# Attention followed by soft MoE and an MLP on one core: remainder-chunk sums and v product as 64x64 corner products, with the maxima and VectorE's long steps spread over other groups

## The chip, the cores and the metric

One core of a Trainium2 chip runs the whole program in one launch. The metric is device time in microseconds (us); lower is better. Times of this kernel differ from run to run by about 0.3%.

## The reference

Only the attention at the front is touched by the change; what follows it (a soft mixture of experts and a two-layer MLP) is unchanged.

```python
def _attn_ref(q, k, v):                   # (4, 8, 576, 64): batch, heads, sequence, head dim
    q_rot, k_rot = rotate(q), rotate(k)   # rotary embedding
    scores = 1/sqrt(64) * q_rot @ k_rot.T
    scores = scores - max(scores, -1)
    attn = exp(scores)
    attn = attn / (sum(attn, -1) + 1e-9)
    return attn @ v
```

All in float32. The attention's output, transposed to (2304, 512), goes into the MoE, and that one's output into the MLP.

## The kernel before

The 32 heads are taken as 16 **pairs** p, each of two heads hd. The 576 query columns of a pair are taken in two **halves** h of 288. The 576 keys of each head make four chunks of 128, and the two remainders of 64 keys (one a head) are put together into one more chunk of 128 rows, the **remainder chunk**, c = 4: rows 0 to 63 are the first head's, rows 64 to 127 the second's. The attention is thus a list of 16 x 2 x 5 = 160 **groups** (p, h, c), with c in the order 4, 0, 1, 2, 3. I number the ten groups of a pair i = 0 to 9: i = 0 is the remainder chunk of the first half, i = 1 to 4 its four whole chunks, i = 5 the remainder chunk of the second half, i = 6 to 9 its whole chunks.

For each group the loop issues, in this order:

- `scores` (L380 to L404): TensorE makes the transposed scores st (keys on the partitions, 288 queries) in float32r, two products for each head (L398 and L399; for the remainder chunk L387 and L388, twice), and ScalarE takes the exponential into the tile e (L400; er, L389, for the remainder chunk). Three PSUM buffers hold st.
- A **maximum unit** (`max_unit`, `max_reduce`, L335 to L361). The maximum of each query's scores is needed before the exponentials, so it is found two pairs ahead: nine units u = 0 to 8 for a pair. A unit is a product with the difference of the two halves of the keys (kd, made by `k_diff`, L335, on VectorE), a relu on ScalarE (L351), a product with the second half of the keys, and one VectorE step (L360) that adds the two and reduces them to a maximum. Each of the two products has one PSUM buffer (mx0, mx1): the next unit's first product must wait for ScalarE's relu, its second for VectorE's step. Unit 4 has two products in place of each. `MAX_AT` says how many units stand in each of the ten groups from group 40 on; before that `MAX_COUNTS` does.
- `esum` (L405 to L417): GpSimd (POOL) adds up e of the four whole chunks into es (L412, then L417 twice), and, with c = 1, the remainder chunk: its rows 0 to 63 onto the first head's (L414), rows 64 to 127 onto the second's (L415).
- `session`: at i = 0 and 5 the product with v, `pv` (L419 to L427), of the chunks 4, 0 and 1 of the half before; at i = 2 and 7 that of the chunks 2 and 3, and then `sums` (L431 to L439), products of es with ones that put each query's sum s on 64 partitions. Products of whole chunks are 128 x 64 (L426, L435): one for each head, with 64 columns of the array each, in float32, which shows as two records for each product. The product of the remainder chunk with v is 128 x 128, with zeros in the two corners that would mix the heads (L423).
- the tasks that a table puts at this group (`at`, `first`): the normalization `norm` (L446, L447, with `NORM`) and `norm2` (L453), the transposed output `x_t` (L465, `X_T`), the rotary steps of a later pair (`ROT`, in order f0 and f1 products L270 and L273, f2 sum L276, f3 rounding L280, m0 copies by DMA, f4 difference L285, m2), `k_diff` (`K_DIFF`), weight conversions (L149 to L155), loads. f0, f2 and f4 run on VectorE, one step a head, f1 on POOL.

All engines run their instructions in the order in which they were issued, so this order is the schedule.

Of the kernel before, what the change touches and what calls it, by code (L numbers as in the profile page):

```python
# [12 lines left out]
ALU = mybir.AluOpType  # L13
# [25 lines left out]
ROT_2 = (-26, -22, -19, -21, -23, -19, -19, -18, -18, -18, -17, -18, -17)  # L39
ROT_3 = (-31, -25, -27, -26, -26, -24, -23, -23, -22, -16, -22, -19, -15)  # L40
ROT_4 = (-28, -28, -26, -28, -24, -23, -23, -20, -22, -17, -19, -21, -17)
ROT = (-28, -27, -24, -24, -24, -23, -22, -22, -21, -20, -20, -19, -19)
Q_COPY = -6
V_LOAD = -6
K_DIFF_2 = -14
K_DIFF_3 = -15
K_DIFF_4 = -16
K_DIFF = -17
QK_LOAD = -34
QK_LOAD_3 = -54  # L50
QK_LOAD_4 = -31
# [2 lines left out]
MAX_ROW_2 = -4  # L54
MAX_ROW_3 = -5
RECIP = 7
NORM = 8
NORM2 = 9
X_T = ((21, 25), (15, 20), (15, 20), (15, 20))
W_IN_AT = (9, 20, 30, 40, 49, 60, 70, 81, 89, 100, 110, 120)  # L60
W_IN_STEPS = (1, 2, 5)
FETCH_AHEAD = 5
# [1 line left out]
W_LOADS = (30, 52, 62, 70, 65, 81, 81, 74, 105, 95, 118, 135, 127, 143, 127, 132, 133, 134, 140, 153)  # L64
SCALES = -19
EARLY = -10
MAX_AT = (0, 1, 1, 1, 1, 1, 1, 1, 1, 1)
MAX_FROM = (6, 2, 6)
MAX_COUNTS = (0, 1, 2, 2, 2, 2, 0, 0, 1, 1, 1, 1, 1, 2, 2, 0, 1, 1, 1, 1, 1, 1, 1, 1, 1, 2, 1, 1, 1, 1, 1, 1, 1, 1, 2, 1, 1, 1, 1, 1)

# [5 lines left out]
def attn_softmoe_mlp_kernel(ctx: ExitStack, tc: tile.TileContext, qk, v, cst, phi, w1, w2, w_in, w_out, out):  # L76
    nc = tc.nc
    pe, act, dve, pool, sp = nc.tensor, nc.scalar, nc.vector, nc.gpsimd, nc.sync
# [13 lines left out]
    ones = const.tile([128, 64], F32, tag="ones", name="ones")  # L92
# [99 lines left out]
    with tc.manual_schedule():  # L192
        with ExitStack() as t1:
# [25 lines left out]
            raw, vt = {}, {}  # L219
# [156 lines left out]
            et = {}  # L376
            u_ps = {}
# [27 lines left out]
            es = {}  # L405

            def esum(p, h, c):
                e = et[p, h, c]
                add = (dve if p == NPAIR - 1 and h == 1 else pool).tensor_tensor
                if c == 1:  # L410
                    t = es[p, h] = (p1 if h else es0).tile([128, 2, HS], F32, tag="es", name=f"es{p}_{h}")
                    add(out=t, in0=et[p, h, 0], in1=e, op=ALU.add)  # L412
                    r = et[p, h, 4]
                    add(out=t[0:64, 0], in0=t[0:64, 0], in1=r[0:64], op=ALU.add)  # L414
                    add(out=t[64:128, 1], in0=t[64:128, 1], in1=r[64:128], op=ALU.add)  # L415
                elif c in (2, 3):
                    add(out=es[p, h], in0=es[p, h], in1=e, op=ALU.add)  # L417

            def pv(p, h, c):  # L419
                e = et[p, h, c]  # L420
                if c == 4:
                    u_ps[p, h] = ps_u.tile([128, HS], F32, tag="u", name=f"u{p}_{h}")
                    pe.matmul(u_ps[p, h], lhsT=vt[p][:, 4, :], rhs=e, start=True, stop=False, skip_group_check=True)  # L423
                    return
                for hd in range(2):
                    pe.matmul(u_ps[p, h][64 * hd:64 * hd + 64, :], lhsT=vt[p][:, c, 64 * hd:64 * hd + 64], rhs=e[:, hd],  # L426
                              start=False, stop=c == 3, skip_group_check=True)  # L427
# [3 lines left out]
            def sums(p, h):  # L431
                wp, tag = (ps_mx, "mx1") if (p, h) == (NPAIR - 1, 1) else (ps_m, "m")
                s = wp.tile([128, HS], F32, tag=tag, name=f"s{p}_{h}", **({"bufs": 1} if wp is ps_mx else {}))
                for hd in range(2):
                    pe.matmul(s[64 * hd:64 * hd + 64, :], lhsT=ones, rhs=es[p, h][:, hd], start=True, stop=True)  # L435
                rs[p, h] = p1.tile([128, HS], F32, tag="rs", name=f"rs{p}_{h}")
                r0[p, h] = p1.tile([128, HS], F32, tag="r0", name=f"r0{p}_{h}")
                act.activation(out=rs[p, h], in_=s, func=ACTF.Ln, bias=eps)
                es[p, h] = s  # L439
# [4 lines left out]
            def norm(p, h):  # L444
                r, q, s = rs[p, h], r0.pop((p, h)), es.pop((p, h))
                dve.scalar_tensor_tensor(out=s, in0=s, scalar=EPS, in1=q, op0=ALU.add, op1=ALU.mult)  # L446
                dve.scalar_tensor_tensor(out=r, in0=s, scalar=-2.0, in1=q, op0=ALU.add, op1=ALU.mult)  # L447
# [179 lines left out]
            def at(g, *fs):  # L627
                tasks.setdefault(g, []).extend(fs)

            def first(g, f):  # L630
                tasks.setdefault(g, []).insert(0, f)
# [33 lines left out]

            ROTARY = [([r[i] for r in (ROT_2, ROT_3, ROT_4, ROT)], k, a) for i, (k, a) in enumerate(((8, ()), (0, (0,)), (1, (0,)), (1, (1,)), (0, (1,)), (2, (0,)), (2, (1,)), (3, (0, act)), (3, (1, act)), (5, ()), (4, (0,)), (4, (1,)), (6, ())))]

            for p in range(NPAIR):
                g0 = 10 * p
                if p >= 1:  # L670
                    at(g0 + Q_COPY, rt(p, 7))
                if p >= 2:
                    for o, k, a in ROTARY:
                        at(g0 + o[min(p, 5) - 2], rt(p, k, *a))
                    at(g0 + V_LOAD, lambda p=p: load_v(p))
                    first(g0 + (K_DIFF_2, K_DIFF_3, K_DIFF_4, K_DIFF)[min(p, 5) - 2], lambda p=p: k_diff(p))
                if p >= 3:
# [8 lines left out]
                    at(g0 + 11, lambda: hb.append(half(1)), lambda: hb[3][0]((0, 1, 2)))  # L686
                for h in range(2 * (p < NPAIR - 1)):
                    first(g0 + 5 * h + RECIP, lambda p=p, h=h: recip(p, h))
                    at(g0 + 5 * h + NORM, lambda p=p, h=h: norm(p, h))
                    at(g0 + 5 * h + NORM2, lambda p=p, h=h: norm2(p, h))  # L690
                for i in range(2 * (p < NPAIR - 1)):
                    at(g0 + X_T[p % 4][i], lambda p=p, i=i: x_t(p, i))
# [77 lines left out]
            g0, g1, g2, g3, g4 = rot[1][0:5]  # L770
# [38 lines left out]
            for g in range(NG + 2):  # L809
                i = g % 10  # L810
                if g < NG:
                    p, h, c = groups[g]
# [35 lines left out]
            t = ps_u.tile([128, HS], F32, tag="u", name="lt3_ps")  # L848
# [43 lines left out]
        op = {}  # L892
# [227 lines left out]
    with tc.manual_schedule():  # L1120
        (wf0, _), (wf1, n1) = first
        dummy(1)
        t = ps_o.tile([128, 512], F32, tag="o", name="g0_ps")[:, 0:128]
# [23 lines left out]
    for n, (j, k) in enumerate(seq):  # L1147
        ghi, glo = gt.pop((j, k))
        for i in range(NI):
            if k == 0:  # L1150
                ops[j, i] = ps_o.tile([128, DM], F32, tag="o", name=f"ops{j}_{i}")
            t = ops[j, i]
# [61 lines left out]
```

## Time and profile before

| | |
|---|---|
| time, median of 3 runs | 689.65 us (688.49 to 690.51) |
| time of the profiled execution | 687.64 us |
| its span, all instructions | 685.8 us |
| mean granted TensorE clock | 0.95 |
| attention's first remainder exponential to its last group | about 27 us to 386 us of the span |
| busy: TensorE, VectorE, ScalarE, POOL | 611.0, 413.4, 360.9, 280.8 us |

The profile is one execution of the program. Busy time counts a matmul up to the end of its pipeline, so TensorE can be counted busy while its array already stands free. A granted clock of 1 is 2.4 GHz, 0.5 is 1.2 GHz. "[0.41 <-ACT relu L351]" behind a row says that the engine stood idle for 0.41 us before it and that ScalarE's step of line 351 ended this.

### The profile page before, as it was taken

What the parts mean: (1) busy time and instruction counts of PE and PEld (TensorE: products, weight loads), DVE (VectorE), ACT (ScalarE), POOL (GpSimd) and SP (SyncE); (2) the same over time, 40 slices, a digit from 0 to 9 for tenths busy, and PEclk for the clock granted to TensorE, in tenths of its full rate; (3) what the DMA queues carried; (4) which work ended last, traced back from release to release, by engine and by line L of the source; (5) the groups of instructions that cost most, each with busy time, mean ns of one, the idle gap of its engine ahead of it and who ended that gap; (6) DMA issues with size and microseconds to landing.
All of it is one profiled execution on the core that took longest, in us unless ns stands there. A gap on an engine that the chain in (4) does not pass through costs nothing.

```text
span 685.8 us, 10364 instructions
## 1 busy us (share of the span) xinstructions
PE 611.0 (89%) x3443; PEld 422.1 (62%) x3443; DVE 413.4 (60%) x866; ACT 360.9 (53%) x920; POOL 280.8 (41%) x226
## 2 busy tenths in 40 slices
PE   4688879889889789888998999998889999999997
PEld 2465655566556456555665533366668888888886
DVE  6686667785577666677824424267895544454443
ACT  2464655674566456466755522068775443454432
POOL 5476587966577665778747200001340000000000
PEclk9579999998799988999999999999999999999999
DMA  6885668865869775577696369983430200020002
GB/s 211 208 228 154 177 174 223 226 168 181 221 181 246 236 207 151 189 193 214 162 328 232 115 246 387 392 331 125 155 99 1 93 0 1 0 93 1 0 1 92
DMA packets 43190, 113.86 MB, mean 166 GB/s; under 512 B 4977, under 2 KB 6273, under 8 KB 41345
## 3 DMA queue, kind: packets, MB, share of 16 engines
q1 hardware_dynamic: 42956, 112.87, 54.1%
q8 instruction: 27, 0.44, 0.3%
q10 hardware_dynamic: 180, 0.34, 0.2%
q14 instruction: 27, 0.21, 0.1%
HBM read 78.12 MB, written 7.60 MB: 125 GB/s over the span
## 4 chain that ended last, share of the span: by engine, by line
PE 63%; DVE 14%; ACT 9%; issue 7%; DMA 5%; ACTq 1%; POOL 1%; SPq 0%; DVEq 0%; POOLq 0%
PE u L426 9%; PE ops L1155 8%; PE ops L1156 8%; PE ops L1154 8%; PE psmx L346 6%; PE st L398 4%; PE l L899 3%; PE st L399 3%; DVE raw L270 2%; ACT relu L351 2%; DVE relu L360 2%; PE s L435 2%; DMA w_out_raw<-in_w_out_dram 2%; PE l L878 2%; PE hps L1049 2%
## 5 line engine op out<-in xcount | busy, mean ns | idle before, releaser
L360 DVE CUSTOM_DVE_ANT_0 relu<-psmx,relu 128x288 f32<-128x288 f32 x144 | 65.2, 454 | 99.7 <-ACT relu L351 75.8
L400 ACT ACTIVATE e<-st 128x288 f32<-128x288 f32 x256 | 101.5, 410 | 23.5 <-PE st L399 22.3
L1155 PE MATMUL ops<-wo_lo,ghi 128*128 128x512 f32 x288 | 112.3, 390 | 0.5 <-POOL wo_lo L1032 0.5
L1154 PE MATMUL ops<-wo_hi,ghi 128*128 128x512 f32 x288 | 112.7, 392 | 0.0
L1156 PE MATMUL ops<-wo_hi,glo 128*128 128x512 f32 x288 | 112.5, 391 | 0.0
L417 POOL TENSOR_TENSOR es<-es,e 128x576 f32<-128x576 f32 x62 | 102.9, 1660 | 9.4 <-ACT e L400 5.0
L1056 DVE TENSOR_TENSOR hps<-hps,g 128x384 f32<-128x384 f32 x96 | 49.9, 560 | 81.5 <-ACT g L1053 81.3
L398 PE MATMUL st<-sa,sa 128*128 128x288 f32 x256 | 88.4, 347 | 1.0 <-ACT er L389 0.6
L1053 ACT ACTIVATE g<-hps 128x384 f32<-128x384 f32 x96 | 42.6, 490 | 81.8 <-PE hps L1049 81.4
L426 PE MATMUL u<-e,v 128*64 128x288 f32 x512 | 85.5, 457 | 0.0
L412 POOL TENSOR_TENSOR es<-e,e 128x576 f32<-128x576 f32 x31 | 45.1, 1456 | 92.5 <-ACT e L400 92.4
L399 PE MATMUL st<-qb,kb 65*128 65x288 f32 x256 | 78.9, 310 | 0.0
L346 PE MATMUL psmx<-sa,sa 128*128 128x288 f32 x160 | 55.2, 362 | 25.0 <-DVE mx L360 24.9
L351 ACT ACTIVATE relu<-psmx 128x288 f32<-128x288 f32 x144 | 58.8, 410 | 29.1 <-DVE mx L360 20.6
L346 PE MATMUL psmx<-kd,sa 128*128 128x288 f32 x160 | 54.3, 356 | 22.0 <-ACT relu L351 14.8
L398 PEld LDWEIGHTS st<-sa,sa 128*128 128x128 f32 x256 | 51.8, 202 | 20.0 <-issue 15.8
L1156 PEld LDWEIGHTS ops<-wo_hi,glo 128*128 128x128 f32 x288 | 54.1, 188 | 11.7 <-issue 0.2
L1155 PEld LDWEIGHTS ops<-wo_lo,ghi 128*128 128x128 f32 x288 | 54.1, 188 | 10.6 <-POOL wo_lo L1032 0.8
L1154 PEld LDWEIGHTS ops<-wo_hi,ghi 128*128 128x128 f32 x288 | 54.0, 188 | 9.6 <-issue 0.2
L1032 POOL TENSOR_TENSOR wo_lo<-wf,wo_hi 128x512 fp32r<-128x512 f32 x14 | 20.1, 1437 | 89.1 <-DMA w_out_raw<-in_w_out_dram 51.5
L426 PEld LDWEIGHTS u<-e,v 128*64 128x64 f32 x512 | 33.3, 148 | 34.6 <-issue 22.8
L346 PEld LDWEIGHTS psmx<-kd,sa 128*128 128x128 f32 x160 | 32.4, 209 | 35.3 <-ACT relu L351 26.5
(191 smaller groups left out, 1072.5 us busy)
## 6 DMA issues: line engine op xcount, KB each, us to landing
w<-in_w_dram SPq DMA_DIRECT2D x64, 512.0 KB
sa<-raw SPq DMA_DIRECT2D x56, 288.0 KB
raw<-in_qk_dram SPq DMA_DIRECT2D x13, 1152.0 KB
w_out_raw<-in_w_out_dram SPq DMA_DIRECT2D x16, 512.0 KB
w_in_raw<-in_w_in_dram SPq DMA_DIRECT2D x12, 512.0 KB
v<-in_v_dram SPq DMA_DIRECT2D x15, 320.0 KB
qb<-sa SPq DMA_DIRECT2D x16, 288.0 KB
out_dram<-os SPq DMA_DIRECT2D x18, 256.0 KB
```

What stands on the lines that cost most here:

```text
L346: pe.matmul(t, lhsT=rem_cols(qa, hd, 128) if u == 4 else qa[:, c0:c0 + 128], rhs=k, start=u != 4 or hd == 0, stop=u != 4 or hd == 1)
L351: act.activation(out=r, in_=t, func=ACTF.Relu)
L360: dve.tensor_tensor_reduce(out=r, in0=mxt.pop((p, u, 1)), in1=r, scale=1.0, scalar=-3.0e38, op0=ALU.add, op1=ALU.max, accum_out=mx[p][:, u ...
L398: pe.matmul(st, lhsT=ka[:, c0:c0 + 128], rhs=qa[:, o:o + HS], start=True, stop=False)
L399: pe.matmul(st, lhsT=kb[0:65, c0:c0 + 128], rhs=qb[0:65, S * hd + HS * h:S * hd + HS * h + HS], start=False, stop=True)
L400: act.activation(out=e[:, hd], in_=st, func=ACTF.Exp, scale=0.125)
L417: add(out=es[p, h], in0=es[p, h], in1=e, op=ALU.add)
L426: pe.matmul(u_ps[p, h][64 * hd:64 * hd + 64, :], lhsT=vt[p][:, c, 64 * hd:64 * hd + 64], rhs=e[:, hd], start=False, stop=c == 3, skip_grou ...
L1056: dve.tensor_tensor(out=t[i], in0=t[i], in1=g[i], op=ALU.mult)
L1154: pe.matmul(t, lhsT=a, rhs=wo_hi[k], start=k == 0, stop=False)
L1155: pe.matmul(t, lhsT=a, rhs=wo_lo[k], start=False, stop=False)
L1156: pe.matmul(t, lhsT=b, rhs=wo_hi[k], start=False, stop=k == 15)
```

## The change

Three things change. The remainder chunk no longer goes through POOL's adds: its sums are two more products in `sums`, each 64 x 64, from rows 0 to 63 to partitions 0 to 63 and from rows 64 to 127 to partitions 64 to 127, accumulated onto those of es. The remainder chunk's product with v becomes two 64 x 64 products in the same corners. And numbers in the tables move: the group without a maximum unit is i = 4 and no longer i = 0, `norm` of the first half goes to i = 9 from i = 8, `k_diff` to i = 4 from i = 3, the second `x_t` to one group later, and of the rotary steps f0 of the first head goes from i = 3 to i = 5, f1 of the first head from i = 6 to i = 5, m0 from i = 0 to i = 9.

```diff
-ROT = (-28, -27, -24, -24, -24, -23, -22, -22, -21, -20, -20, -19, -19)
+ROT = (-28, -25, -25, -24, -24, -23, -22, -22, -21, -21, -20, -19, -19)
...
-K_DIFF = -17
+K_DIFF = -16
...
-NORM = 8
+NORM = (9, 8)
 NORM2 = 9
-X_T = ((21, 25), (15, 20), (15, 20), (15, 20))
+X_T = ((21, 25), (15, 21), (15, 21), (15, 21))
...
-MAX_AT = (0, 1, 1, 1, 1, 1, 1, 1, 1, 1)
+MAX_AT = (1, 1, 1, 1, 0, 1, 1, 1, 1, 1)
...
                     add(out=t, in0=et[p, h, 0], in1=e, op=ALU.add)
-                    r = et[p, h, 4]
-                    add(out=t[0:64, 0], in0=t[0:64, 0], in1=r[0:64], op=ALU.add)
-                    add(out=t[64:128, 1], in0=t[64:128, 1], in1=r[64:128], op=ALU.add)
...
-                    pe.matmul(u_ps[p, h], lhsT=vt[p][:, 4, :], rhs=e, start=True, stop=False, skip_group_check=True)
+                    for r in (slice(0, 64), slice(64, 128)):
+                        pe.matmul(u_ps[p, h][r, :], lhsT=vt[p][r, 4, r], rhs=e[r], start=True, stop=False, skip_group_check=True)
...
                 for hd in range(2):
-                    pe.matmul(s[64 * hd:64 * hd + 64, :], lhsT=ones, rhs=es[p, h][:, hd], start=True, stop=True)
+                    pe.matmul(s[64 * hd:64 * hd + 64, :], lhsT=ones, rhs=es[p, h][:, hd], start=True, stop=False, skip_group_check=True)
+                for r in (slice(0, 64), slice(64, 128)):
+                    pe.matmul(s[r, :], lhsT=ones[r], rhs=et[p, h, 4][r], start=False, stop=True, skip_group_check=True)
...
-                    at(g0 + 5 * h + NORM, lambda p=p, h=h: norm(p, h))
+                    at(g0 + 5 * h + NORM[h], lambda p=p, h=h: norm(p, h))
```

Where instructions now stand, at three places of a pair in the middle of the attention (p = 10 to 12; the name relu12_6 is unit 6 of the maxima of pair 12, an ISA row with relu in it is VectorE's maximum step, raw13 and raw14 are the rotary input of pairs 13 and 14).

VectorE from i = 3 to i = 5, before:

```order
L360 ISA relu12_6_3261,mx12_3092<-psmx12_6_1_3267,relu12_6_3261 128x288
L360 ISA mx12_3092 128x1
L335 TENSOR_TENSOR kd1_152<-sa1_1_143 128x576
L446 SCALAR_TENSOR_TENSOR s10_1_3246<-s10_1_3246,r010_1_3250 128x288
L447 SCALAR_TENSOR_TENSOR rs10_1_3249<-s10_1_3246,r010_1_3250 128x288
L270 TENSOR_TENSOR raw14_3102<-raw14_3102,tab_139 128x576
L360 ISA relu12_7_3282,mx12_3092<-psmx12_7_1_3288,relu12_7_3282 128x288
L360 ISA mx12_3092 128x1
L453 SCALAR_TENSOR_TENSOR xt10_3174<-u10_1_3184,rs10_1_3249 128x288
L360 ISA relu12_8_3305,mx12_3092<-psmx12_8_1_3307,relu12_8_3305 128x288
```

VectorE at the same place, after the change:

```order
L360 ISA relu12_7_3288,mx12_3112<-psmx12_7_1_3294,relu12_7_3288 128x288
L360 ISA mx12_3112 128x1
L446 SCALAR_TENSOR_TENSOR s10_1_3271<-s10_1_3271,r010_1_3277 128x288
L447 SCALAR_TENSOR_TENSOR rs10_1_3276<-s10_1_3271,r010_1_3277 128x288
L335 TENSOR_TENSOR kd1_152<-sa1_1_143 128x576
L453 SCALAR_TENSOR_TENSOR xt10_3193<-u10_1_3215,rs10_1_3276 128x288
L360 ISA relu12_8_3324,mx12_3112<-psmx12_8_1_3326,relu12_8_3324 128x288
L360 ISA mx12_3112 128x1
L270 TENSOR_TENSOR raw14_3121<-raw14_3121,tab_139 128x576
```

Unit 6 of before is unit 7 now, so that only unit 8 is left for i = 5; between the maxima of units 7 and 8, `k_diff` (L335) now stands behind `norm`, and the rotary product (L270) has gone behind the maximum of unit 8.

VectorE from i = 8 to i = 9, before:

```order
L360 ISA relu12_2_3143,mx12_3092<-psmx12_2_1_3149,relu12_2_3143 128x288
L360 ISA mx12_3092 128x1
L446 SCALAR_TENSOR_TENSOR s10_0_3128<-s10_0_3128,r010_0_3132 128x288
L447 SCALAR_TENSOR_TENSOR rs10_0_3131<-s10_0_3128,r010_0_3132 128x288
L276 TENSOR_TENSOR raw13_2835<-raw13_2835 128x576
L360 ISA relu12_3_3164,mx12_3092<-psmx12_3_1_3170,relu12_3_3164 128x288
L360 ISA mx12_3092 128x1
```

VectorE from i = 8 to i = 0, after:

```order
L360 ISA relu12_2_3162,mx12_3112<-psmx12_2_1_3168,relu12_2_3162 128x288
L360 ISA mx12_3112 128x1
L276 TENSOR_TENSOR raw13_2852<-raw13_2852 128x576
L360 ISA relu12_3_3181,mx12_3112<-psmx12_3_1_3187,relu12_3_3181 128x288
L360 ISA mx12_3112 128x1
L446 SCALAR_TENSOR_TENSOR s10_0_3145<-s10_0_3145,r010_0_3151 128x288
L447 SCALAR_TENSOR_TENSOR rs10_0_3150<-s10_0_3145,r010_0_3151 128x288
L453 SCALAR_TENSOR_TENSOR xt10_3193<-u10_0_3074,rs10_0_3150 128x288
L360 ISA relu12_4_3209,mx12_3112<-psmx12_4_1_3211,relu12_4_3209 128x288
L360 ISA mx12_3112 128x1
```

`norm` (L446, L447) has gone behind the maximum of unit 3, so that the rotary sum (L276) follows the maximum of unit 2 directly, and the maximum of unit 4 comes already at i = 0.

TensorE at i = 0, from the remainder chunk's scores to the product with v, before:

```order
L387 MATMUL st11_0_r_3178<-sa2_0_144,sa2_1_145 128x288
L388 MATMUL st11_0_r_3178<-qb1_150,kb2_148 128x288
L387 MATMUL st11_0_r_3178<-sa2_0_144,sa2_1_145 128x288
L388 MATMUL st11_0_r_3178<-qb1_150,kb2_148 128x288
L423 MATMUL u10_1_3184<-er10_1_3043,v10_2768 128x288
L426 MATMUL u10_1_3184<-e10_1_0_3077,v10_2768 64x288 x2
L426 MATMUL u10_1_3184<-e10_1_1_3104,v10_2768 64x288 x2
```

TensorE at i = 0, after:

```order
L387 MATMUL st11_0_r_3200<-sa2_0_144,sa2_1_145 128x288
L388 MATMUL st11_0_r_3200<-qb1_150,kb2_148 128x288
L387 MATMUL st11_0_r_3200<-sa2_0_144,sa2_1_145 128x288
L388 MATMUL st11_0_r_3200<-qb1_150,kb2_148 128x288
L346 MATMUL psmx12_4_0_3206<-kd0_151,sa0_0_140 128x288 x2
L346 MATMUL psmx12_4_1_3211<-sa0_1_141,sa0_0_140 128x288 x2
L421 MATMUL u10_1_3215<-er10_1_3060,v10_2783 64x288 x2
L424 MATMUL u10_1_3215<-e10_1_0_3097,v10_2783 64x288 x2
L424 MATMUL u10_1_3215<-e10_1_1_3123,v10_2783 64x288 x2
```

Unit 4's four products now stand between the scores and the product with v, which begins with the 64 x 64 products; L421 and L424 are the changed kernel's lines for L423 and L426.

## Rows read from the trace of the kernel before

**Rows 1.** Busy time of each engine by stretch: start:end, length, PE, PEld, DVE, ACT, POOL, clock.

```profile
27.43:103.31 75.88, 60.28 (x313) 41.66 (x312) 52.45 (x107) 42.02 (x112) 53.05 (x38) 0.84 0.70 189
103.31:333.68 230.37, 200.95 (x1220) 133.21 (x1219) 160.10 (x343) 138.19 (x388) 163.49 (x121) 0.93 0.72 200
333.68:386.00 52.32, 48.43 (x316) 31.59 (x316) 22.67 (x62) 31.26 (x91) 30.88 (x26) 1.00 0.80 254
291.33:312.29 20.96, 17.58 (x113) 12.01 (x112) 15.68 (x34) 13.08 (x38) 16.33 (x13) 1.00 0.76 220
251.50:261.70 10.20, 10.20 (x45) 6.06 (x43) 4.43 (x12) 2.46 (x7) 5.62 (x5) 0.50 0.62 210
```

**Rows 2.** Waits of TensorE from 103.31 to 333.68 us: total, times, longest.

```profile
PE psmx L346 <- DVE mx L360: 17.8, 10, 3.1
PE psmx L346 <- ACT relu L351: 10.5, 27, 0.6
```

**Rows 3.** Timeline of TensorE, the wait at i = 5.

```profile
298.54 0.30 PE L346 MATMUL psmx<-kd,sa 128*128 128x288 f32 x1
300.82 0.40 PE L346 MATMUL psmx<-sa,sa 128*128 128x288 f32 x1 [1.99 <-DVE mx L360]
```

**Rows 4.** Timeline of VectorE at the same place.

```profile
297.63 0.88 DVE L335 TENSOR_TENSOR kd<-sa 128x576 fp32r<-128x576 f32 x1
298.43 0.45 DVE L446 SCALAR_TENSOR_TENSOR s<-s,r 128x288 f32<-128x288 f32 x1
...
299.29 1.10 DVE L270 TENSOR_TENSOR raw<-raw,tab 128x576 f32<-128x576 f32 x1
300.31 0.45 DVE L360 CUSTOM_DVE_ANT_0 relu<-psmx,relu 128x288 f32<-128x288 f32 x1
```

**Rows 5.** Timeline of TensorE ahead of a fall of the clock, at i = 5.

```profile
250.99 0.40 PE L346 MATMUL psmx<-sa,sa 128*128 128x288 f32 x1 [1.38 <-DVE mx L360]
```

**Rows 6.** Timeline of TensorE around the products with v and ones.

```profile
284.13 0.29 PE L399 MATMUL st<-qb,kb 65*128 65x288 f32 x1
284.26 0.40 PE L346 MATMUL psmx<-sa,sa 128*128 128x288 f32 x1
284.58 1.19 PE L426 MATMUL u<-e,v 128*64 128x288 f32 x8
285.61 0.66 PE L435 MATMUL s<-es,ones 128*64 128x288 f32 x4
...
288.44 0.40 PE L346 MATMUL psmx<-sa,sa 128*128 128x288 f32 x1
...
289.21 0.65 PE L423 MATMUL u<-er,v 128*128 128x288 f32 x2
289.79 1.19 PE L426 MATMUL u<-e,v 128*64 128x288 f32 x8
```

**Rows 7.** Timeline of TensorE where 64-row products follow 128-row ones.

```profile
169.02 1.06 PE L518 MATMUL sps<-x,d 128*32 128x512 f32 x8
170.02 0.42 PE L521 MATMUL sps<-x,d 64*32 64x128 f32 x8
```

**Rows 8.** Timeline of VectorE, POOL and ScalarE from i = 7 to i = 1.

```profile
285.18 1.91 DVE L276 TENSOR_TENSOR raw<-raw 128x576 f32<-128x576 f32 x1
287.91 0.46 DVE L360 CUSTOM_DVE_ANT_0 relu<-psmx,relu 128x288 f32<-128x288 f32 x1 [0.82 <-ACT relu L351]
...
293.44 0.75 DVE L285 TENSOR_TENSOR raw<-raw 128x576 f32<-128x576 f32 x1
...
285.08 1.40 POOL L412 TENSOR_TENSOR es<-e,e 128x576 f32<-128x576 f32 x1 [3.68 <-ACT e L400]
...
287.77 0.41 ACT L400 ACTIVATE e<-st 128x288 f32<-128x288 f32 x1
```

**Rows 9.** Groups of the page: POOL's adds of the remainder chunk.

```profile
L414 POOL TENSOR_TENSOR es<-es,er 64x288 f32<-64x288 f32 x31 | 33.3, 1075 | 2.4
L415 POOL TENSOR_TENSOR es<-es,er 64x288 f32<-64x288 f32 x31 | 25.6, 825 | 1.8
```

## The prediction

> **What bounds the kernel now.** I read the stretches of the span first, then TensorE's waits in the stretch that matters, then the timeline at one wait of each kind. In the attention TensorE is the busiest engine in every stretch [rows 1]; behind 386 us the change touches nothing. Between 103.31 us (pair 3) and 333.68 us (pair 13) it is counted busy for 200.95 of 230.37 us, a pair taking 23.0 us, and its mean granted clock is 0.93: part of that stretch ran at 1.2 GHz. In the last three pairs, which have little rotary work, it is busy for 48.43 of 52.32 us at a clock of 1.00. So the attention is bound by TensorE with holes in it, and an instruction added to TensorE is paid in full except where it falls into a hole.
>
> The holes of the middle stretch are of two kinds [rows 2]. Ten waits, 17.8 us in all, are for VectorE's maximum. They stand at i = 5, where two units' products follow each other closely: the second product of unit 8 needs the PSUM buffer that VectorE's maximum of unit 7 must first read [rows 3], and VectorE is at `k_diff`, `norm` and f0 then, in a row from 297.63 us until that maximum starts at 300.31 [rows 4]. The other 27, 10.5 us in all, are for ScalarE's relu, about 0.39 us each; ten stand at i = 4, behind the sums, where ScalarE is late by its logarithm and reciprocal.
>
> The holes also cost clock. After the wait of 1.38 us that ended at 250.99 us [rows 5], TensorE ran at 0.50, that is at 1.2 GHz, from 251.50 to 261.70 us, and was busy all the time [rows 1]. A mean of 0.93 over 230.37 us is 0.07 x 230.37 = 16.1 us of full-clock work not done. The pair from 291.33 to 312.29 us has a wait of 1.99 us too [rows 3] and stays at 1.00 [rows 1], so a fall also depends on how the waits lie.
>
> **What is removed.** POOL's two adds a half, 33.3 + 25.6 = 58.9 us [rows 9]. I count nothing for it: POOL has waits of 3.68 us for ScalarE's exponentials in between [rows 8], and the sums follow its last add by a run of other products. If they did wait, removing the adds would gain.
>
> **What TensorE gets.** A float32 product pair of 288 columns, one for each head, shows as two passes; four pairs of products fill 284.58 to 285.61 us [rows 6], eight records in 1.03 us, so two records beside each other cost 0.24 to 0.26 us, and one set of two corner products costs 0.48 us if the corners run beside each other as the column halves do.
>
> In `sums` the set is new: 0.48 us. In `pv` it replaces a full product of two records, which took 0.58 us from 289.21 to 289.79 us with the change to 64 columns behind it. Entering 64 columns directly costs what lies between 284.26 and 284.58 us, 0.32 less the usual 0.13 between two products (284.13 to 284.26), so 0.19 us, and some 0.05 in the first pass.
>
> Whether 64 rows behind 128 rows stop the array is seen at one place only: products of 128 x 32 and 512 columns, followed by 64 x 32 ones, stand at 169.02 and 170.02 us [rows 7]. Two passes of 512 columns are 2 x 0.24 x 512 / 288 = 0.86 us, so 0.14 us went into the change of rows. Each run of 64 columns gets one more such change; I take 0.12 us. `pv` then costs 0.19 + 0.05 + 0.48 + 0.12 - 0.58 = +0.26 us a half, `sums` 0.48 + 0.12 = +0.60, together **+0.86 us a half**. Without a stop at the change of rows it is 0.57; with the corners one after the other it is 0.86 + 2 x 0.48 = 1.82. These are the ends.
>
> Of the 32 halves, 20 lie in the middle stretch (17.2 us) and 6 in the last three pairs (5.2 us). For the 6 of the first three pairs I count half (2.6 us), since 15.6 of those 75.88 us are idle on TensorE [rows 1]. Sum: **+25.0 us**.
>
> **What the new places do.** Without a unit at i = 4, unit 7 is at i = 3, and VectorE's maximum of it comes before `norm` and `k_diff`. So the ten waits go: -17.8 us, and 0.17 each on top, since a product counts as busy for 0.30 us [rows 3] but the next could start after 0.13: **-19.5 us**. Late next at this place is ScalarE, whose exponentials must free the score buffers; that may give back up to the 0.56 us of the next term, and is kept for the range. The relu wait at i = 4 has no product left to hold up: 10 x (0.39 + 0.17) = **-5.6 us**.
>
> At i = 0 stands unit 4 now, right behind unit 3's maximum, and there a wait is new. VectorE finishes the maximum of unit 2 at about 288.30 us [rows 8] and goes straight to the rotary sum f2, which took 1.91 us where a POOL add had begun 0.10 us before it, while a step of the same size alone takes 0.75 [rows 8]. Then comes the maximum of unit 3 (0.46). TensorE has passed unit 3's product at 288.44 [rows 6], has four score products (0.13 each) and unit 4's first two to do, and asks at about 289.5. VectorE is ready at 289.5 without POOL and 290.7 with it, and ScalarE's relu puts the first case at about 289.8: a wait of 0.3 to 1.1 us. (The corner products move all of these by the same amount.) The POOL add is now freed by the exponential that ends at 288.18 [rows 8], ahead of f2 by about 0.05 us, so I take a value nearer the upper end, 0.8, for ten pairs: **+8 us**.
>
> The other moves: `k_diff` at i = 4 is still two groups ahead of the first unit that needs it; f0 and f1 come at i = 5, two groups ahead of f2; m0's DMAs are issued one group earlier on SP's queue, behind the rounding that they wait for in any case; `norm` at i = 9 holds the sums' PSUM buffer a group longer, for which `x_t` was moved. Nothing each; the price if a cover is gone is some 1 us in the three pairs in which the MoE's slot sums take that buffer at i = 0.
>
> **Clock.** With the longest regular wait falling from 1.99 to 0.8 us I expect most falls to stay away: **-13 us** of the 16.1. Ends: 0 and -16.1.
>
> Sum: 25.0 - 19.5 - 5.6 + 8 - 13 = **-5.1 us**, on the profiled execution's 687.64 us. The median of the three runs, 689.65 us, is 2.0 us above that execution; the forecast for it is 689.65 - 5.1 = **684.5 us**. A difference under 0.3% (2.1 us) can't be told from none here.
>
> **A rule against it.** No row shows products of two different row halves at once; the nearest are the two column halves in rows 6, which do overlap, and that is why I take overlap. The Trainium skill, "TensorEngine Tiling (Array Packing)", section "Restrictions and Gotchas", says that different row tiles write to different PSUM banks and can't access the same one at the same time. Both corners here write one buffer, on different partitions; by that rule each set would go one after the other, and the sum would be that of the first rival below. The trace neither bears it out nor contradicts it.
>
> **Rivals.**
>
> *The corners go one after the other.* Then each set takes 0.96 us, +0.96 a half, over 29 counted halves +28 us: **712.5 us**, slower. It decides from 5.1 / 29 = 0.18 us a half on: that much more, and nothing is gained. For it: no row of this trace shows row halves together. Against it: the column halves and the four column quarters [rows 6, 7] run in parallel, and the corners share neither rows nor columns. Chance 0.13.
>
> *VectorE's wait moves to i = 0 and the clock goes on falling.* The new wait is 1.1 us every time (+3) and, with the relu wait at i = 9 just ahead of it, pulls the clock down as often as the old one (+13): 684.5 + 16 = **700 us**; with half of the falls, 694 us. For it: 1.38 us was enough once [rows 5]. Against it: the pair from 291.33 us had 1.99 us without a fall [rows 1, 3]. Chance 0.17.
>
> *The wait at i = 5 stays.* `k_diff`'s input copies or ScalarE's place in between keep VectorE late, and half of the 19.5 us remains: **694 us**. This is the change not doing what its numbers are for. Chance 0.10, since the order shows the maximum of unit 7 ahead of all three long steps.
>
> *Better than forecast.* f2 gets in before POOL's add (wait 0.3, -5 us), the change of rows costs nothing (0.29 x 29 = -8 us): **671 us**. Chance 0.15.
>
> **Chances and range.** The forecast's own case, 0.45, reaches from 677 to 690 us: clock ends of +-3 to 5 us and the waits' ends. The range that should hold the time 8 times in 10 reaches down to 671 and up to 700 us; what is left out is the serial case and little below. Faster by over 0.3% (below 687.6 us): most of the forecast's case, all of the better one and a little of the third, 0.53. Slower by over 0.3% (above 691.7 us): the serial case, nearly all of the second and third rival, 0.32. Within: 0.15.
>
> **What would show it.** Right: the corner rows come in pairs 0.24 us apart; the sums' run is longer by 0.6 us; TensorE's waits for VectorE's maximum drop from 17.8 to about 8 us, and stand at i = 0; the stretch's clock is at 0.98 or more. Wrong: corner rows 0.24 us apart one by one, waits at i = 5 of over 1 us, or a clock still at 0.93. If the clock stays and all the rest holds, the time is 697 us.

## The result and the profile after

The changed kernel takes **672.0 us** (670.18 to 673.83, four runs) beside 689.85 us for the kernel before in the same session: ratio 0.9744, 95% interval 0.9707 to 0.978. The time is 17.8 us shorter where 5.1 were forecast; it lies inside the forecast's range, near its lower end. Times below are medians of executions within 1.5% of the fastest of the same kernel; only the last experiment had others, two of ten (696.14 and 697.75 us).

The changed kernel's profiled execution took 670.18 us. Of its page, the span, the busy times and TensorE's granted clock in 40 slices:

```profile
span 668.4 us, 10697 instructions
PE 620.1 (93%) x3635; PEld 416.3 (62%) x3635; DVE 406.8 (61%) x864; ACT 355.7 (53%) x920; POOL 229.0 (34%) x164
PEclk9689999999999999999999999998999999999999
```

The span is 17.4 us shorter, although TensorE is busy for 9 us more than before; POOL is busy for 52 us less. Behind the third slice the clock is nearly everywhere at its higher level.

The stretches of the changed kernel, in the columns of [rows 1] (length; busy time of PE, PEld, DVE, ACT and POOL; clock; DMA share; GB/s). The first two begin and end at the same instructions as the first two of [rows 1]; the third goes on to 397.45 us of before, the fourth is all that follows:

```profile
27.39:96.85 69.46, 58.53 (x343) 38.91 (x342) 49.23 (x105) 41.13 (x111) 39.66 (x25) 0.93 0.75 201
96.85:310.19 213.34, 204.22 (x1329) 127.36 (x1330) 156.88 (x343) 134.44 (x388) 132.71 (x81) 1.00 0.78 218
310.19:378.86 68.67, 65.81 (x454) 37.77 (x454) 28.98 (x81) 37.38 (x109) 23.24 (x17) 1.00 0.62 193
378.86:668.40 289.54, 275.29 (x1461) 202.42 (x1461) 153.01 (x300) 132.52 (x297) 20.73 (x15) 0.99 0.33 120
```

The same cut of the kernel before, for the two stretches that [rows 1] does not have:

```profile
333.68:397.45 63.77, 59.47 (x402) 35.93 (x400) 29.45 (x81) 37.92 (x109) 30.88 (x26) 1.00 0.65 208
397.45:685.80 288.35, 274.06 (x1461) 201.55 (x1461) 152.84 (x300) 132.48 (x297) 20.71 (x15) 1.00 0.33 120
```

| stretch | before | after | measured | forecast |
|---|---|---|---|---|
| first three pairs | 75.88 | 69.46 | -6.4 | +2.6 |
| middle ten pairs | 230.37 | 213.34 | -17.0 | -12.9 |
| last three pairs and the start of the MoE | 63.77 | 68.67 | +4.9 | +5.2 |
| the rest | 288.35 | 289.54 | +1.2 | 0 |
| sum | | | -17.3 | -5.1 |

So the forecast missed 9 us in the first three pairs and 4 in the middle, in the same direction. In the middle stretch two things can be read off the rows: TensorE's busy time rose by 3.3 us (200.95 to 204.22), and its idle time fell by 20.3 (29.42 to 9.12). That busy time rose by so little with all the new products in it goes with the clock, 0.93 before and 1.00 now.

TensorE's waits in the middle stretch of the changed kernel (total, times, longest), the answer to [rows 2]:

```profile
PE psmx L346 <- ACT relu L351: 4.9, 13, 0.4
...
PE psmx L346 <- DVE mx L360: 0.7, 2, 0.3
PE xps L465 <- DVE xt L453: 0.5, 1, 0.5
```

The ten waits for VectorE's maximum at i = 5 are gone, and the new ones forecast for i = 0 did not come. Why not is to be seen at i = 9 and i = 0. TensorE there, from unit 3's first product to the product with v (start, duration, product; L421 and L424 are the changed kernel's products with v, L433 and L435 its sums):

```profile
262.68 1.19 PE L424 MATMUL u<-e,v 128*64 128x288 f32 x8
263.70 0.66 PE L433 MATMUL s<-es,ones 128*64 128x288 f32 x4
264.29 0.70 PE L435 MATMUL s<-er,ones 64*64 64x288 f32 x4
264.92 0.40 PE L398 MATMUL st<-sa,sa 128*128 128x288 f32 x1
...
268.14 0.53 PE L346 MATMUL psmx<-kd,sa 128*128 128x288 f32 x2
268.64 0.53 PE L346 MATMUL psmx<-sa,sa 128*128 128x288 f32 x2
269.10 0.70 PE L421 MATMUL u<-er,v 64*64 64x288 f32 x4
269.73 1.19 PE L424 MATMUL u<-e,v 128*64 128x288 f32 x8
```

Unit 4's second products (268.64) follow its first without a wait. VectorE at the same place, then POOL, then ScalarE:

```profile
266.65 0.46 DVE L360 CUSTOM_DVE_ANT_0 relu<-psmx,relu 128x288 f32<-128x288 f32 x1 [1.00 <-ACT relu L351]
...
267.03 0.75 DVE L276 TENSOR_TENSOR raw<-raw 128x576 f32<-128x576 f32 x1
268.12 0.46 DVE L360 CUSTOM_DVE_ANT_0 relu<-psmx,relu 128x288 f32<-128x288 f32 x1 [0.34 <-PE st_r L388]
...
267.06 3.50 POOL L414 TENSOR_TENSOR es<-es,e 128x576 f32<-128x576 f32 x2 [2.03 <-ACT e L400]
...
266.21 0.40 ACT L351 ACTIVATE relu<-psmx 128x288 f32<-128x288 f32 x1
266.50 0.41 ACT L400 ACTIVATE e<-st 128x288 f32<-128x288 f32 x1
```

The rotary sum f2 (L276) began at 267.03 us, POOL's add of a whole chunk (L414 here, L417 in the kernel before) at 267.06. Being first by 0.03 us, f2 took 0.75 us and not 1.91 as in [rows 8], and VectorE even waited for the next maximum's input. The order is the same in all ten pairs of the stretch, by 0.03 us each time, and the rows show why: VectorE's maximum waits for ScalarE's relu (over at 266.61 us), and POOL's add for the exponential right behind that relu (over at 266.91). POOL's add begins 0.15 us after that, and by then the maximum is done and f2 has begun.

The sums and the products with v also show the corners' price. The four records of two corner products, with the change of shape, take 0.63 us from 264.29 to 264.92 and again from 269.10 to 269.73.

### The profile page after: what moved, and what is told of

Same layout as the page of the kernel before. It is cut to its first block, busy times and chain, and to the rows that moved or that the text cites. A ratio compares the mean times of both kernels' runs of the same rounds, so it can differ in the third digit from the quotient of the medians.

```text
span 668.4 us, 10697 instructions
## 1 busy us (share of the span) xinstructions
PE 620.1 (93%) x3635; PEld 416.3 (62%) x3635; DVE 406.8 (61%) x864; ACT 355.7 (53%) x920; POOL 229.0 (34%) x164
## 4 chain that ended last, share of the span: by engine, by line
PE 71%; DVE 8%; ACT 8%; issue 6%; DMA 5%; SPq 1%; POOL 1%; ACTq 0%; DVEq 0%; POOLq 0%
PE u L424 10%; PE ops L1155 8%; PE ops L1156 8%; PE ops L1154 8%; PE psmx L346 8%; PE st L398 4%; PE st L399 3%; PE l L899 3%; PE u L421 3%; PE s L435 3%; PE l L878 2%; DMA w_out_raw<-in_w_out_dram 2%; PE hps L1049 2%; ACT e L400 2%; PE s L433 2%
## 5 line engine op out<-in xcount | busy, mean ns | idle before, releaser
L414 POOL TENSOR_TENSOR es<-es,e 128x576 f32<-128x576 f32 x62 | 100.0, 1612 | 66.8 <-ACT e L400 60.2
L360 DVE CUSTOM_DVE_ANT_0 relu<-psmx,relu 128x288 f32<-128x288 f32 x144 | 65.0, 453 | 89.6 <-ACT relu L351 79.0
L424 PE MATMUL u<-e,v 128*64 128x288 f32 x512 | 77.1, 420 | 0.0
L399 PE MATMUL st<-qb,kb 65*128 65x288 f32 x256 | 76.4, 300 | 0.0
L412 POOL TENSOR_TENSOR es<-e,e 128x576 f32<-128x576 f32 x31 | 48.3, 1556 | 70.4 <-ACT e L400 70.3
L346 PE MATMUL psmx<-kd,sa 128*128 128x288 f32 x160 | 52.7, 346 | 14.9 <-ACT relu L351 8.2
L351 ACT ACTIVATE relu<-psmx 128x288 f32<-128x288 f32 x144 | 59.5, 415 | 13.0 <-PE psmx L346 6.6
L398 PEld LDWEIGHTS st<-sa,sa 128*128 128x128 f32 x256 | 49.3, 193 | 24.8 <-issue 18.5
L346 PE MATMUL psmx<-sa,sa 128*128 128x288 f32 x160 | 52.5, 345 | 5.9 <-DVE mx L360 5.5
L273 POOL TENSOR_TENSOR raw<-raw,tab 128x576 f32<-128x576 f32 x31 | 53.2, 1733 | 13.6 <-DMA raw<-in_qk_dram 13.6
L1062 DVE TENSOR_TENSOR glo<-hps,ghi 128x384 fp32r<-128x384 f32 x96 | 49.6, 551 | 5.3 <-ACT ghi L1059 2.0
L1059 ACT ACTIVATE ghi<-hps 128x384 fp32r<-128x384 f32 x96 | 45.7, 492 | 11.0 <-DVE hps L1056 11.0
```

What stands on the lines that cost most here:

```text
L273: eng.tensor_tensor(out=r[:, hd, 1], in0=r[:, hd, 1], in1=c(1), op=ALU.mult)
L346: pe.matmul(t, lhsT=rem_cols(qa, hd, 128) if u == 4 else qa[:, c0:c0 + 128], rhs=k, start=u != 4 or hd == 0, stop=u != 4 or hd == 1)
L351: act.activation(out=r, in_=t, func=ACTF.Relu)
L360: dve.tensor_tensor_reduce(out=r, in0=mxt.pop((p, u, 1)), in1=r, scale=1.0, scalar=-3.0e38, op0=ALU.add, op1=ALU.max, accum_out=mx[p][:, u ...
L398: pe.matmul(st, lhsT=ka[:, c0:c0 + 128], rhs=qa[:, o:o + HS], start=True, stop=False)
L399: pe.matmul(st, lhsT=kb[0:65, c0:c0 + 128], rhs=qb[0:65, S * hd + HS * h:S * hd + HS * h + HS], start=False, stop=True)
```

## The experiments

Each kernel was timed against the kernel before, in two sessions after the changed kernel's own: the kernel before took 689.85 us beside the changed kernel, 691.55 beside the tables alone, the corners alone, the full rows and the maxima's place, and 689.65 beside the others. A difference of medians from two sessions is therefore good only to about 2 us. The theory under test: the tables alone gain far more than the whole change, the corners take part of it back, and f2's place ahead of POOL's add decides whether a new wait arises at i = 0. The rival: the gain comes from POOL, which the change frees of its adds of the remainder chunk.

### The tables alone

The kernel before with all the new numbers, and its old products and POOL adds:

```diff
-ROT = (-28, -27, -24, -24, -24, -23, -22, -22, -21, -20, -20, -19, -19)
+ROT = (-28, -25, -25, -24, -24, -23, -22, -22, -21, -21, -20, -19, -19)
-K_DIFF = -17
+K_DIFF = -16
-NORM = 8
+NORM = (9, 8)
-X_T = ((21, 25), (15, 20), (15, 20), (15, 20))
+X_T = ((21, 25), (15, 21), (15, 21), (15, 21))
-MAX_AT = (0, 1, 1, 1, 1, 1, 1, 1, 1, 1)
+MAX_AT = (1, 1, 1, 1, 0, 1, 1, 1, 1, 1)
```

> The tables' new numbers alone: POOL's adds of the remainder chunk and the full 128x128 product with v stay. Theory A (the table moves take VectorE's and ScalarE's waits away and with them the clock's falls; the corner products only cost TensorE about 0.87 us a half; POOL's adds matter only in the first three pairs): the middle stretch without waits and without the 17 us of corner products, the first three pairs as before: about 656 us, granted clock 1.00 in the middle stretch. Rival B (POOL's adds are what makes VectorE late, by holding it up; without their removal the moves don't help): waits for VectorE's maximum of over 10 us remain in the middle stretch, clock still 0.93 to 0.95, 680 to 690 us.

Measured: **654.25 us** (652.12 to 658.1), ratio 0.9473, interval 0.9427 to 0.9519. It is the fastest kernel of this study that computes everything, 17.75 us faster than the whole change. Its first and middle stretches, and then TensorE's longest waits in the middle one:

```profile
28.00:94.59 66.59, 56.15 (x313) 38.97 (x313) 52.59 (x105) 41.35 (x111) 51.94 (x37) 0.90 0.73 196
94.59:295.84 201.25, 188.59 (x1209) 124.86 (x1209) 166.92 (x343) 134.91 (x387) 170.75 (x121) 1.00 0.83 234
```

```profile
PE psmx L346 <- ACT relu L351: 4.9, 13, 0.4
PE psmx L346 <- DVE mx L360: 1.5, 3, 0.7
PE xps L465 <- DVE xt L453: 1.3, 1, 1.3
PE st_r L388 <- DMA qb<-m: 1.1, 1, 1.1
PE psmx L346 <- ACT e L400: 1.0, 1, 1.0
```

The middle stretch is 29.1 us shorter than before: 16.8 of them idle time of TensorE (29.42 to 12.66) and 12.4 busy time (200.95 to 188.59, with the same work to do, at a clock of 1.00 in place of 0.93; there are 21 fewer waits in the rows of lines L360 and L351, and by the prediction's count of 0.17 us for a product that a wait follows up to 3.6 of the 12.4 are the ends of such products and not the clock). POOL still does its adds here (170.75 us busy), so the rival falls. The expectation had the first three pairs as before and gave POOL's adds a part there; with the adds still in place they are 9.3 us shorter. The time came out near the expected 656 us, but not by the way that was expected.

The difference to the whole change is the corners' price: 12.1 us in the middle stretch, namely 15.6 us more of busy time and 3.5 us less of idle time. The waits of the last four rows, 4.9 us here, are 1.2 in the changed kernel (its last two rows above), which is the 3.5 within the rounding of the rows.

### The corners alone

The changed kernel with all tables as before (the diff above, reversed).

> The corner products alone, with the old tables. Theory A: TensorE gets 0.87 us a half on top and keeps its waits at i = 5 and the falls of the clock in the middle stretch; only the first three pairs gain, some 6 us as in the changed kernel: 700 to 708 us. Rival B (POOL's adds were the cause): the waits at i = 5 shrink to under half, the clock is at 0.98 or more in the middle stretch, and the time is 680 us or less.

Measured: 699.81 us (698.64 to 704.52), ratio 1.0139, interval 1.009 to 1.0187. By the ratios the corners cost 9.6 us with the old tables, and 18.7 with the new (17.75 by the medians). Its first and middle stretches, and its largest wait in the latter:

```profile
26.27:102.86 76.59, 61.85 (x342) 40.52 (x342) 52.72 (x109) 41.72 (x112) 40.39 (x26) 0.89 0.71 192
102.86:340.66 237.80, 211.66 (x1338) 131.16 (x1337) 156.11 (x343) 137.62 (x388) 126.63 (x81) 0.95 0.70 194
```

```profile
PE psmx L346 <- DVE mx L360: 16.0, 10, 2.9
```

The waits at i = 5 stand as before (17.8 us there), so freeing POOL does nothing for them. Busy time is 10.7 us up and the stretch 7.4, so 3.3 us fell into holes; with the new tables it is 3.5, no less. The lower price comes with the clock: it is 0.95 here, where it was 0.93, and 0.02 of the stretch is some 5 us, what separates 10.7 from the 15.6 us of busy time that the same products add at a clock of 1.00. Why the clock is higher with the corners was not tried. The expected gain of 6 us in the first three pairs did not come either: they are 0.7 us longer than before.

### No adds and no corners

The tables alone, with the remainder chunk left out of the sums; nothing takes its place, so this kernel leaves out part of the computation.

```diff
-                    r = et[p, h, 4]
-                    add(out=t[0:64, 0], in0=t[0:64, 0], in1=r[0:64], op=ALU.add)
-                    add(out=t[64:128, 1], in0=t[64:128, 1], in1=r[64:128], op=ALU.add)
```

> The tables' new numbers with POOL's adds of the remainder chunk left out and nothing in their place: the softmax's sums lack the remainder chunk. This is the price of POOL's adds by themselves, 58.9 us of its busy time. If they lie beside other work, the time is that of the tables alone, 652 to 656 us. If they hold VectorE or the sums up, 648 us or less.

Measured: 652.04 us (647.9 to 653.19), ratio 0.9445, interval 0.9399 to 0.9492. Its middle stretch:

```profile
94.59:295.47 200.88, 188.40 (x1209) 124.95 (x1210) 159.25 (x343) 135.13 (x387) 131.57 (x81) 1.00 0.84 235
```

POOL is busy for 131.57 us in place of 170.75, and the stretch is 0.4 us shorter. The two medians differ by 2.2 us, with intervals that overlap: POOL's adds of the remainder chunk cost 2 us at most, and moving them to TensorE bought no more than that for its 17.75 us.

### Full rows in place of corners

The changed kernel with the corners as 128 x 64 products: for v the columns of one head, whose other half of rows is zero already, and for the sums a tile of ones with zeros in that half. The arithmetic adds only zeros.

```diff
-                        pe.matmul(u_ps[p, h][r, :], lhsT=vt[p][r, 4, r], rhs=e[r], start=True, stop=False, skip_group_check=True)
+                        pe.matmul(u_ps[p, h][r, :], lhsT=vt[p][:, 4, r], rhs=e, start=True, stop=False, skip_group_check=True)
...
-                for r in (slice(0, 64), slice(64, 128)):
-                    pe.matmul(s[r, :], lhsT=ones[r], rhs=et[p, h, 4][r], start=False, stop=True, skip_group_check=True)
+                for hd in range(2):
+                    pe.matmul(s[64 * hd:64 * hd + 64, :], lhsT=hones[:, hd], rhs=et[p, h, 4], start=False, stop=True, skip_group_check=True)
```

> The changed kernel with the corners as 128x64 products: the weights are v's remainder chunk with its zeros, and a tile of ones with zeros in the other head's rows, so that no run changes from 128 to 64 rows. Same number of passes. If the change of rows stops the array by 0.12 to 0.15 us each time, as the one place in the trace of before and the 0.10 us gaps ahead of and behind the corner rows in the trace after suggest, two fewer changes a half save 0.24 to 0.29 us on each of 29 to 32 halves: 663 to 665 us. If a 64-row product costs nothing in itself, 671 to 673 us.

Measured: 665.0 us (663.14 to 666.33), ratio 0.9617, interval 0.9573 to 0.9661: 7.0 us less than the changed kernel. TensorE's products with v and the sums (lines shifted by 4):

```profile
254.75 0.71 PE L425 MATMUL u<-er,v 128*64 128x288 f32 x4
255.29 1.14 PE L428 MATMUL u<-e,v 128*64 128x288 f32 x8
...
260.82 0.66 PE L437 MATMUL s<-es,ones 128*64 128x288 f32 x4
261.30 0.66 PE L439 MATMUL s<-er,hones 128*64 128x288 f32 x4
261.89 0.40 PE L402 MATMUL st<-sa,sa 128*128 128x288 f32 x1
```

From the first row of each run, 0.54 us (254.75 to 255.29) stand against 0.63 (269.10 to 269.73) for v, and 1.07 (260.82 to 261.89) against 1.22 (263.70 to 264.92) for the sums: 0.24 us a half, or 7.7 over 32 halves. No fewer products are computed; what goes is the change of the array's rows. It was forecast at 0.12 us for each of the two runs; they save 0.09 and 0.15.

### The maxima's place undone

```diff
-MAX_AT = (1, 1, 1, 1, 0, 1, 1, 1, 1, 1)
+MAX_AT = (0, 1, 1, 1, 1, 1, 1, 1, 1, 1)
```

> The changed kernel with MAX_AT as before (no unit at i = 0, one at i = 4), all else new. If the place of the maximum units is what takes the wait at i = 5 away: waits for VectorE's maximum of 1 us and more come back at i = 5, with falls of the clock, 690 us or more. If moving the VectorE steps (norm, k_diff, f0) is enough: the wait at i = 5 stays under 0.4 us, only ScalarE's relu wait at i = 4 comes back, 0.56 us a pair: about 678 us, clock 1.00.

Measured: 672.19 us (671.35 to 677.02), ratio 0.9741, interval 0.9693 to 0.9789: no difference to the whole change, and the expectation missed. Its first and middle stretches, and its waits in the latter:

```profile
27.05:98.64 71.59, 60.78 (x343) 40.24 (x342) 48.58 (x105) 41.18 (x112) 39.34 (x25) 0.88 0.75 198
98.64:311.98 213.34, 201.48 (x1332) 127.67 (x1334) 155.41 (x343) 136.06 (x387) 128.49 (x81) 0.99 0.78 218
```

```profile
PE psmx L346 <- ACT relu L351: 8.6, 22, 0.4
PE psmx L346 <- DVE mx L360: 1.9, 6, 0.8
```

The waits for ScalarE's relu come back, 8.6 us in place of 4.9, and the stretch is as long to the hundredth. TensorE is busy for 2.7 us less here (201.48 and 204.22) and idle for 2.7 us more: what the new place of the units saves in waits it costs in busy time. Which products pay for it was not followed.

The first three pairs are issued exactly as in the changed kernel, since `MAX_AT` counts from group 40 on; yet they took 71.59 us at a clock of 0.88, and 69.46 at 0.93 there. So that stretch differs by 2 us between executions.

### Which of the moved steps

Two kernels take one part of the tables each, from the kernel before. The normalization's place alone (`NORM`, `X_T`):

```diff
-NORM = 8
+NORM = (9, 8)
-X_T = ((21, 25), (15, 20), (15, 20), (15, 20))
+X_T = ((21, 25), (15, 21), (15, 21), (15, 21))
```

> The kernel before with NORM and X_T alone as in the change (norm of the first half behind unit 3's maximum). If the wait at i = 5 is made by k_diff, norm of the second half and f0 standing there, which this leaves, the middle stretch keeps 14 to 18 us of waits for VectorE's maximum and a clock of 0.93 to 0.95, and only the first three pairs can gain: 683 to 691 us. If norm's place is what made VectorE late, under 670 us.

The rotary steps and `k_diff` alone:

```diff
-ROT = (-28, -27, -24, -24, -24, -23, -22, -22, -21, -20, -20, -19, -19)
+ROT = (-28, -25, -25, -24, -24, -23, -22, -22, -21, -21, -20, -19, -19)
-K_DIFF = -17
+K_DIFF = -16
```

> The kernel before with ROT and K_DIFF alone as in the change (f0 behind unit 8's maximum, k_diff one group later). If these two steps make the wait at i = 5, the waits for VectorE's maximum in the middle stretch fall under 4 us, the clock is 0.99 or more there, and most of the gain of all tables is here: 657 to 666 us. If the place of the maximum units or norm is needed as well, 675 us or more.

Measured: 682.44 us for the first, a little below what was expected (679.71 to 685.55; ratio 0.9884, 0.9837 to 0.993), 660.85 for the second (659.13 to 665.18; ratio 0.9594, 0.9543 to 0.9644). The middle stretch and the waits for VectorE's maximum in it, of the normalization's place alone:

```profile
100.27:328.37 228.10, 200.91 (x1210) 134.00 (x1212) 158.44 (x343) 137.91 (x388) 163.70 (x121) 0.92 0.73 202
```

```profile
PE psmx L346 <- DVE mx L360: 17.0, 9, 3.1
```

and of the rotary steps and `k_diff` alone:

```profile
102.53:305.17 202.64, 189.06 (x1220) 125.94 (x1219) 162.90 (x343) 137.23 (x387) 173.89 (x121) 0.99 0.82 229
```

```profile
PE psmx L346 <- DVE mx L360: 3.5, 8, 1.6
```

In the middle stretch the second part is nearly the whole: with f0 and `k_diff` out from between the maxima of units 7 and 8, the waits fall from 17.8 to 3.5 us and the stretch from 230.37 to 202.64; with all tables it is 201.25. (f1 and m0 go with f0 in this kernel; none of the four was tried apart.) Here the normalization still stands ahead of f2, but no unit stands at i = 0 to wait for what follows.

### The normalization put back in the changed kernel

```diff
-NORM = (9, 8)
+NORM = (8, 8)
```

> The changed kernel with norm of the first half back ahead of f2, at i = 8. f2 then starts some 0.9 us later, after POOL's add has begun, and takes 1.5 to 2 us where it took 0.75; the maximum of unit 3 is late, and unit 4's second product at i = 0 waits. This is the wait that was forecast as 0.8 us a pair and did not come: if the forecast was wrong only because f2 got in ahead of POOL's add, it comes here, 0.8 to 1.5 us in ten pairs: 680 to 688 us, more if the clock falls. If unit 4 does not hang on f2, 671 to 674 us.

Measured: **688.27 us** (685.23 to 693.14, eight runs), ratio 0.9982, interval 0.995 to 1.0014. One number of a table takes back 16.3 of the 17.8 us. Its middle stretch and the waits in it for VectorE's maximum:

```profile
101.20:328.11 226.91, 209.33 (x1329) 128.90 (x1329) 158.83 (x343) 135.44 (x387) 130.82 (x81) 0.98 0.73 204
```

```profile
PE psmx L346 <- DVE mx L360: 10.1, 13, 0.9
```

And one of these waits at i = 0, on VectorE, POOL and TensorE:

```profile
257.06 0.46 DVE L446 SCALAR_TENSOR_TENSOR s<-s,r 128x288 f32<-128x288 f32 x1
257.55 0.46 DVE L447 SCALAR_TENSOR_TENSOR rs<-s,r 128x288 f32<-128x288 f32 x1
257.93 1.21 DVE L276 TENSOR_TENSOR raw<-raw 128x576 f32<-128x576 f32 x1
...
257.09 3.32 POOL L414 TENSOR_TENSOR es<-es,e 128x576 f32<-128x576 f32 x2 [2.02 <-ACT e L400]
...
259.56 0.53 PE L346 MATMUL psmx<-sa,sa 128*128 128x288 f32 x2 [0.88 <-DVE mx L360]
```

With the normalization ahead of it again, f2 begins 0.84 us after POOL's add, takes 1.21 us, and unit 4's second products wait 0.88 us for the maximum behind it. Eleven of the 13 waits are of this kind, 0.84 to 0.88 us each; the other two, of 0.3 us, the changed kernel has too. It is a wait at the place and of the size that the prediction gave, but not by its way alone: f2 begins 0.87 us later because the normalization stands ahead of it (257.06 to 257.93), and takes 0.46 us longer because of POOL's add (1.21 against 0.75; 1.5 to 2 were expected). What the order of f2 and the add is worth with the normalization behind them was not tried.

## Why the prediction was wrong, and where it was right

**The step that failed.** The prediction gave the moved tables no part in the first three pairs, and no reason for it: the only term for that stretch is half of the corners' price, +2.6 us. The stretch became 6.4 us shorter. That is 9.0 of the 12.2 us by which the forecast missed; the tables alone took 9.3 us out of it. The second step is the corners' price in the middle stretch, 17.2 us forecast and 12.1 measured.

**The tables in the middle stretch: right in the sum, in part by luck.** Its four terms, -19.5, -5.6, +8 and -13, make -30.1 us, and -29.1 were measured. But the two removed waits, 25.1 us, show as 16.8 us of idle time, and the new wait of 8 us did not come: two misses of the same size cancel.

**What bounds the kernel.** Right. TensorE with holes bounds the attention; the holes that count are the ten at i = 5, and the steps that were moved away from there made them. They went (17.8 us to 0.7), and with the tables alone the middle stretch became 29.1 us shorter. That POOL's adds count for nothing held too (2.2 us at most).

**"+8 us", the new wait at i = 0: wrong.** The prediction saw that POOL's add and f2 begin within about 0.05 us of each other, and took a value near the upper end, with POOL first. In the profiled execution f2 is first by 0.03 us, and the waits are 0.7 us in all. What it had wrong is the start of the add: 0.05 us ahead of f2's 288.30 is 288.25, that is 0.07 us after the exponential's end at 288.18, and in the changed kernel this add begins 0.15 us after it. That such a wait can arise there, at 0.84 to 0.88 us, the last experiment shows; by how much f2's order alone makes it, no run shows. An order that 0.05 us decide, between no wait and ten of 0.8 us and more, should have been two cases with a chance each, not one term with a value in between.

**The first three pairs, "+2.6 us": wrong, and the largest miss of all.** Half of the corners' price fits (69.46 us with them and 66.59 without), as far as one execution each can tell. But the prediction gave the tables no part in that stretch, though [rows 1] showed a clock of 0.84 and 15.6 us of idle time in it. The tables alone took 9.3 us out, 75.88 to 66.59, and the clock rose to 0.90, in the whole change to 0.93. The cause within that stretch stays partly open: in single profiles the normalization's place alone gives 3.8 us there (72.11 us long), the rotary steps and `k_diff` alone 1.4 (74.45), both together 9.3. The same program's stretch can differ by 2 us between executions (71.59 and 69.46), so no run tells whether the two do more than their sum, or which waits they end there.

**The clock, "-13 us": right.** The middle stretch went from 0.93 to 1.00, which by the prediction's own reckoning is all of its 16.1 us. In TensorE's busy time, with the same work, it shows as 12.4 at most and 8.8 without the 3.6 that can be ends of products.

**"-5.6 us" for the relu waits: wrong.** These waits did fall, from 10.5 to 4.9 us. But with the maxima back in their old places 3.7 us of them return and the time stays the same: the place saves waits and costs as much busy time, which the prediction left out.

**The corners, "+0.86 us a half": right each time, and too high in the sum.** The set costs 0.63 us in the sums and, by the prediction's rule, 0.63 + 0.19 - 0.58 = 0.24 in v: 0.87. (Its lower end, 0.57 without a stop at the change of rows, should be 0.62 by its own terms: 0.86 less two changes of 0.12.) The whole came to 17.75 us, where 25.0 were forecast: in the middle stretch 15.6 us of busy time over 20 halves are 0.78 a half, and 3.5 us fell into holes that the tables had left. The remaining 0.09 a half is not explained.

**The serial rival and the rule behind it.** Four records of 0.24 us each, one after the other, would take 0.96 us; with the change of rows they take 0.63, so the two corners ran beside each other, into one buffer and on different partitions. The rule of the Trainium skill that different row tiles can't access one PSUM bank at once ("TensorEngine Tiling (Array Packing)", "Restrictions and Gotchas") did not bind here. That a change of tiling mode drains the array (the Trainium skill, "TensorEngine Tiling (Array Packing)", "Key Properties") agrees with the 0.24 us a half that full rows save.

**The better rival** named 671 us, and 672.0 came. Its first half was what happened (f2 ahead of POOL's add). Its second was not: full rows save 7.0 us, so the change of rows costs what the forecast said. The rest came from the first three pairs, which this rival did not name either; that its number fits is luck.

## What to carry to other kernels

A step is worth moving when it stands between two of its engine's steps for which the bounding engine asks close to each other; waits of that engine elsewhere may come and go at no price, so test them one by one. Time the parts of a bundle apart: here a few numbers of a table gave 35 us, and the new products, which relieved an engine that nobody waited for, gave 18 of them back. The same products had cost some 10 with the old tables, where the clock still had room to rise with them (0.93 to 0.95): the price of a part depends on what the rest has left. Where products on half of the rows stand within runs on all rows, fill up with zeros if the data allow it: that alone saved 7 us.

## What the runs showed of the hardware

VectorE's step f2 and POOL's add, which both read two inputs in SBUF, stand in each other's way, and the start decides. A step f2 of one head took 0.75 us where it began 0.03 us ahead of POOL's add, 1.21 us where it began 0.84 us behind one, and 1.91 us where it began 0.10 us behind one [rows 8]: the later it comes into the add, the less of it is left to wait for. The Trainium skill says so ("SBUF — State Buffer", "Who interferes with whom": a VectorE instruction with two SBUF inputs contends with a GpSimd instruction that reads SBUF, and issue order decides which one blocks); the three values agree on VectorE's side.

With the normalization put back, eleven waits of 0.84 to 0.88 us go with a granted clock of 0.98 in the middle stretch, where it is 1.00 without them, and TensorE is busy for 5.1 us more with the same work (209.33 and 204.22): some of what the new wait costs is paid at the lower of the two levels, 1.2 GHz.
